# One block of products, one difference, one unit's keys and a range-check step in another place of the order (HGRN2 attention and a maxout FFN on one core)

## The chip, the cores and the metric

The kernel runs on one core of one Trainium2 chip. The metric is the device time of one execution in microseconds (us). The engines named below are PE (TensorE: matmuls, with its weight loads shown apart as PEld), DVE (VectorE), ACT (ScalarE), POOL (GpSimd) and SP (SyncE, which here only issues DMAs).

## The reference, cut to what matters

```python
# q, k, v, f_logit: (4, 8, 768, 48)
f = 1.0 / (1.0 + np.exp(-f_logit))
for t in range(S):
    state = f[:, :, t, :, None] * state + einsum('bhd,bhe->bhde', k[:, :, t], v[:, :, t])
    y[:, :, t] = einsum('bhd,bhde->bhe', q[:, :, t], state)
x = y.transpose(0, 2, 1, 3).reshape(3072, 384)      # tokens x (heads * head_dim)
h = max(max(x @ w1, x @ w2), x @ w3)                # w1..w3: 384 x 768
out = h @ w_out                                     # 768 x 384
```

## The kernel before, in words

**Units and groups.** The attention works in 24 units (u = 0 to 23). A unit is a chunk of 64 time steps of two batches, 128 tokens. Four units make a group of 512 tokens, and there are six groups (g = 0 to 5). The FFN of a group is computed while the attention of the next group runs. `load`, `load_v` and `load_weights` issue the transfers, nearly all on SP's queue.

**One unit of attention.** `sigmoids(u)` makes the gates (ACT). `scan(u)` and `before(u)` run the running products over time (DVE, L329 and L347). `after(u)` and `before(u)` scale keys and queries: `kh` (L340) and `qh` (L351), on DVE for units 0 to 5 and on POOL afterwards. `keys(u)` turns `kh` for the state's sum: for units 0 to 5 that is four PE transposes (L367) into a PSUM bank and an ACT copy to `ks` (L369). For later units `keys_by_blocks` does it on DVE (L382). `pairs(u)` makes the 32 products of keys and queries on PE (L396) and masks them on DVE (L399). `values(u)` multiplies them with v (L415); where u is 4 or more, a tiny ACT copy `seen` (L422) marks that PE is through. `sums(u)` multiplies `ks` with v (L433). `finish(u)` adds the old state's part on PE (L504), which waits for `seen`, and copies the result to the group's `xT` in three ACT copies (L511). `pack` moves pieces of `xT` to other partitions by DMA.

**The FFN in portions.** `fill(ns)` takes steps of the pending FFN generator until their stated cost is used up. So the order on each engine is written out by hand: a few FFN steps, then a step of the attention, and so on. Every engine runs its own instructions in that order.

**The FFN of groups 1 to 5**, `inputs_by_pairs(g, hm, xT)`, works on 256 columns of two weight blocks at once (index n = 0, 1, 2) in the manner of a Winograd-Strassen product, with sums and differences of weights (made once) and of tokens. `sums_of_x(g)` makes the five differences t1 to t5 of tokens on POOL (L865). The steps concerned here all use a helper `into` (L881), whose call makes two 128x256 fp32 matmuls, which the trace shows as four records:

- `start(n)`: one `into` in a new bank A[n] from the pool that the trace calls "p"; ACT copies it to `first` (L895, shown as rest_bits).
- `plain(n)`: two `into` in a new bank B[n] from the pool "tr"; ACT copies it to `out(n, 0)`, columns of `hm` (L889). Both pools have two banks.
- `join(n)`: POOL adds `first` to `out(n, 0)` (L899).
- `sixth(n)`: adds one `into` to A[n]; ACT copies it to `out(n, 1)` (L909).
- `fifth(n)`: starts B[n] anew with one `into`; ACT copies it to a tile `top` (L904).
- `seventh(n)`: adds two `into` to A[n]; ACT copies it (L916, shown as top_bits), POOL adds `top` (L917).
- `third(n)`, `fourth(n)`: further products into B[n] and A[n], read by DVE (L924; L931 and L932).

After them `outputs_by_pairs` makes the output products (L636), with two "tr" banks and one "p" bank. Its last DVE read of a "tr" bank is L644. `store_late()` puts the stores of the group before on SP's queue.

**The FFN of group 0**, `ffn_first`, rounds and prepares the weights as it goes. In its output part it makes four differences of `w_out` columns on POOL: `mix(0)` to `mix(3)` (L592). `mix(1)` overwrites columns of `w_out` that the plain output products of group 0 still read.

**The range check.** From unit 10 on, `check_range(n, step)` checks one loaded weight piece on ACT in three steps: step 0 takes absolute values (L278), steps 1 and 2 compare and add up (L280 and a read of the accumulator). In the loop over units its three steps are spread over the unit's portions.

Of the kernel before, what the change touches and what calls it, by code (L numbers as in the profile page):

```python
# [55 lines left out]
def kernel(  # L56
# [21 lines left out]
    GRP = 4  # L78
# [11 lines left out]
    def fast():  # L90
        ctx = ExitStack()
        with ctx:
# [704 lines left out]
            def ffn_first(xT):  # L797
                hm = new_hm()
                steps = [(j, slice(n * HALF, (n + 1) * HALF)) for n in range(2) for j in range(J_HALF)]
                steps += [(j, slice(0, TOK)) for j in range(J_HALF, NJ)]  # L800
                n_step = 0
                for j, t in steps:
                    w = t.stop - t.start
                    for i in (1, 2):
                        p = yield from product(xT, j, i, t)
                        if i == 1:
                            nc.scalar.copy(hm[:, j, t], p)
                        else:
                            nc.vector.scalar_tensor_tensor(hm[:, j, t], hm[:, j, t], 0.0, p, op0=ALU.max, op1=ALU.max)
                        round_to(ROUNDED[n_step])  # L810
                        load_weights(2, rounded[0] - 1)
                        yield (1 if w == TOK else NK) * w * COLUMN
                        n_step += 1
                        if n_step in TURNED:
                            yield from turn(TURNED[n_step])
                for a in range(NK):
                    if a < 2:
                        for n in range(2 * NK + 2):
                            place(placed[a].bitcast(FP32), w_in[a + 1], n)
                    for cost in linear(a):  # L820
                        round_to(rounded[0] + 1)
                        yield cost
                for n in range(2 * NK + 2):
                    place(w_lin, w_nat, n)
                made = iter([lambda n=n: mix_in(n) for n in range(4)] + [lambda: mix(0)])
                for i in range(GRP):
                    for n, cost in enumerate(outputs(hm, xT, i)):
                        if i or n:
                            next(made, lambda: None)()
                        if i == GRP - 1 and n == 1 and 1 in packed:  # L830
                            sums_of_x(1)
                        if i == GRP - 1 and n == 2:
                            for k in range(1, 4):
                                mix(k)
                        yield cost

# [15 lines left out]
            packed, summed = {}, {}  # L852
# [3 lines left out]
            def sums_of_x(g):  # L856

                if g not in summed:
                    xT = packed[g]
                    X = lambda k, h: halves(xT, k, h)  # L860
                    t1, t2, t3, t4, t5 = (halves(xT, NK, 0), halves(xT, NK, 1), s_mix[0][:, HJ - 1],
                                          rests[:, 2, 0:HALF], s_mix[1][:, HJ - 1])
                    for dst, x, y in ((t1, X(0, 1), X(0, 0)), (t2, X(1, 1), t1), (t3, X(1, 1), X(0, 1)),
                                      (t4, X(1, 0), t2), (t5, X(2, 0), X(2, 1))):
                        nc.gpsimd.tensor_tensor(dst, x, y, op=ALU.subtract)  # L865
                    summed[g] = t1, t2, t3, t4, t5
                return summed[g]

            def inputs_by_pairs(g, hm, xT):
                X = lambda k, h: halves(xT, k, h)  # L870
                t1, t2, t3, t4, t5 = sums_of_x(g)
                s1, s2, s4 = w_sum
                s3 = w_two[1][:, 0]
                COST = 2 * HALF * COLUMN
                out = lambda n, h: hm[:, 2 * n:2 * n + 2, h * HALF:(h + 1) * HALF]
                first, u3 = rests[:, 0:2, 0:HALF], tops[:, 2:4, 0:HALF]
                A, B, U5 = {}, {}, {}

                def into(b, n, w, x, begin=False):
                    for j in range(2):  # L880
                        nc.tensor.matmul(b[:, j * HALF:(j + 1) * HALF], lhsT=w[:, (2 * n + j) * 128:(2 * n + j + 1) * 128],  # L881
                                         rhs=x, start=begin and j == 0, stop=True, skip_group_check=True)

                def plain(n):
                    B[n] = bank(True)
                    into(B[n], n, w_two[0][:, 1], X(1, 0), True)
                    yield COST
                    into(B[n], n, w_two[0][:, 2], X(2, 0))
                    nc.scalar.copy(out(n, 0), two(B[n]))  # L889
                    yield COST  # L890

                def start(n):
                    A[n] = bank()
                    into(A[n], n, w_two[0][:, 0], X(0, 0), True)
                    nc.scalar.copy(first, two(A[n]))  # L895
                    yield COST

                def join(n):
                    nc.gpsimd.tensor_tensor(out(n, 0), out(n, 0), first, op=ALU.add)  # L899

                def fifth(n):
                    into(B[n], n, s1, t1, True)
                    U5[n] = two(new_top(TOK))
                    nc.scalar.copy(U5[n], two(B[n]))  # L904
                    yield COST

                def sixth(n):
                    into(A[n], n, s2, t2)
                    nc.scalar.copy(out(n, 1), two(A[n]))  # L909
                    yield COST  # L910

                def seventh(n):
                    into(A[n], n, s3, t3)
                    yield COST
                    into(A[n], n, w_two[1][:, 2], X(2, 1))
                    nc.scalar.copy(u3, two(A[n]))  # L916
                    nc.gpsimd.tensor_tensor(u3, u3, U5[n], op=ALU.add)  # L917
                    yield COST

                def third(n):  # L920
                    into(B[n], n, s4, X(1, 1))
                    yield COST
                    into(B[n], n, w_two[0][:, 2], X(2, 1))
                    nc.vector.tensor_tensor(out(n, 1), two(B[n]), out(n, 1), op=ALU.add)  # L924
                    yield COST

                def fourth(n):
                    into(A[n], n, w_two[1][:, 1], t4)
                    yield COST
                    into(A[n], n, w_two[1][:, 2], t5)  # L930
                    nc.vector.scalar_tensor_tensor(out(n, 0), out(n, 0), 0.0, two(A[n]), op0=ALU.max, op1=ALU.max)  # L931
                    nc.vector.scalar_tensor_tensor(out(n, 1), out(n, 1), 0.0, u3, op0=ALU.max, op1=ALU.max)  # L932
                    sums_of_hm(hm, n)
                    if g == 1:
                        for i in ((0, 1), (2, 3, 4), ())[n]:
                            mix_x(i)
                    yield COST

                yield from start(0)
                yield from plain(0)  # L940
                join(0)
                store_late()
                yield from sixth(0)
                yield from fifth(0)
                for n in range(1, NJ // 2):
                    yield from plain(n)
                    yield from seventh(n - 1)
                    yield from start(n)
                    join(n)
                    yield from third(n - 1)  # L950
                    yield from fifth(n)
                    yield from sixth(n)
                    yield from fourth(n - 1)
                yield from seventh(NJ // 2 - 1)
                yield from third(NJ // 2 - 1)
                yield from fourth(NJ // 2 - 1)
# [35 lines left out]
            with tc.manual_schedule():  # L992
# [78 lines left out]
                for u in range(GRP, NU):  # L1071
# [2 lines left out]
                    if n == BY_ROWS:  # L1074
                        scan(n)
                    fill(part)
                    keys(u)
                    keys_by_blocks(u, 2)
                    room_of_unit = room_of_pairs()
                    if u > GRP:  # L1080
                        values(u - 1)
                        sums(u - 1, room_of_unit)
                    pairs(u, room_of_unit)
                    if u > GRP:
                        finish(u - 1, xT)
# [17 lines left out]
                    if n < NU:  # L1103
                        if n < BY_ROWS:
                            sigmoids(n)
                        if n != BY_ROWS:
                            scan(n)
                    check_range(u - CHECKS, 0)
                    fill(part)
                    if n < NU:  # L1110
                        after(n)
                        before(n)
                    fill(part)
                    if BY_ROWS < u + 2 < NU and u % GRP == 0:
                        load(u + 2, one, "k")
# [289 lines left out]
```

## Time and profile before

| | us |
|---|---|
| median of 3 runs (lowest to highest) | 415.52 (415.32 to 416.43) |
| the profiled execution | 416.13 |
| its span, first to last instruction | 414.4 |
| PE busy, DVE busy, POOL busy, ACT busy | 393.5, 295.1, 246.0, 180.4 |
| granted PE clock, mean | 0.999 |
| one group in the steady part (182.4 to 241.3, 241.3 to 300.2) | 58.9 |

A busy time adds up an engine's instructions; matmul records overlap, so a busy PE is not a PE at its peak. "Idle before" and "waited for" name the instruction that released the waiting one, as the profile infers it from semaphore events. The "chain" is followed back from the last instruction, at each step to what released it.

### The profile page before, as it was taken

Reading aid. Unit: us, or ns where it says so; the run is one execution under the profiler, and the core shown is the slowest. Engines: PE = TensorE matmul, PEld = TensorE weight load, DVE = VectorE, ACT = ScalarE, POOL = GpSimd, SP = SyncE. Lnnn points to the kernel's source line nnn. Section 1 sums busy time; section 2 is a strip of 40 time slices with the busy share of each in tenths; the row PEclk is TensorE's granted clock in tenths of the full one; section 3 lists DMA queues with packets and bytes.
Section 4 is the critical chain, followed back from the end, with each engine's and each line's share of the span. In section 5 each row is a group of like instructions: output and inputs, shape, how many; then the busy total and the mean of one; then the engine's idle time right before and its main releaser. Section 6 shows DMA issues by size and latency. Waiting matters only on the chain.

```text
span 414.4 us, 11516 instructions
## 1 busy us (share of the span) xinstructions
PE 393.5 (95%) x4598; PEld 331.8 (80%) x4598; DVE 295.1 (71%) x569; ACT 180.4 (44%) x430; POOL 246.0 (59%) x270
## 2 busy tenths in 40 slices
PE   5988999999999989999999999999999999999995
PEld 4766765556667878998889988899988889988994
DVE  6997896997785899898899997998995550002600
ACT  2488786421223522335532345532445424586110
POOL 2189694830969777567495296577377860435700
PEclk9999999999999999999999999999999999999999
DMA  8999886676356766277645276735374003542002
GB/s 168 238 271 272 246 228 90 85 139 161 84 103 99 122 108 124 57 96 114 114 123 109 43 112 85 148 87 89 60 144 110 2 17 88 133 133 72 0 21 62
DMA packets 181562, 47.21 MB, mean 114 GB/s; under 512 B 160448, under 2 KB 179200, under 8 KB 181504
## 3 DMA queue, kind: packets, MB, share of 16 engines
q1 hardware_dynamic: 178032, 45.62, 54.1%
q10 hardware_dynamic: 3472, 0.81, 0.9%
q8 instruction: 37, 0.61, 0.6%
q14 instruction: 21, 0.17, 0.1%
HBM read 37.75 MB, written 4.72 MB: 102 GB/s over the span
## 4 chain that ended last, share of the span: by engine, by line
PE 74%; SPq 6%; POOL 5%; DVE 5%; ACT 4%; issue 2%; DMA 2%; POOLq 0%
PE p L881 15%; PE p L636 14%; PE tr L881 12%; PE tr L636 10%; PE p L542 7%; PE p L568 3%; PE p L787 3%; PE y L415 2%; SPq L164 2%; SPq L174 2%; DVE ks L382 2%; PE y L504 2%; PE a L396 2%; PE a L433 2%; POOL w_in L258 1%
## 5 line engine op out<-in xcount | busy, mean ns | idle before, releaser
L382 DVE STREAM_TRANSPOSE ks<-kh 32x128 f32<-32x128 f32 x256 | 77.4, 302 | 13.4 <-POOL kh L340 9.4
L881 PE MATMUL tr<-xT,placed 128*128 128x256 f32 x300 | 71.5, 383 | 1.1 <-ACT hm L889 1.1
L881 PEld LDWEIGHTS tr<-xT,placed 128*128 128x128 f32 x300 | 56.0, 190 | 10.4 <-ACT hm L889 2.6
L881 PE MATMUL p<-xT,placed 128*128 128x256 f32 x180 | 44.8, 380 | 1.1 <-POOL xT L865 0.8
L339 POOL COPY ends<-r 128x8 f32<-128x8 f32 x24 | 8.8, 366 | 51.1 <-DVE r L329 51.1
L881 PEld LDWEIGHTS p<-xT,placed 128*128 128x128 f32 x180 | 33.9, 190 | 6.4 <-POOL xT L865 1.2
L542 PE MATMUL p<-xT,w_in 128*128 128x256 f32 (+1 forms) x108 | 34.0, 459 | 3.4 <-POOL w_in L756 1.9
L329 DVE TENSOR_TENSOR_SCAN r<-gate,from_one 128x520 f32<-128x520 f32 x24 | 32.5, 1354 | 6.1 <-ACT gate L308 2.8
L340 POOL TENSOR_TENSOR kh<-kt,r 128x512 f32<-128x512 f32 x18 | 30.9, 1715 | 7.6 <-DVE kt L296 7.6
L511 ACT COPY xT<-y 64x256 f32<-64x256 f32 (+1 forms) x60 | 22.1, 368 | 23.2 <-PE y L504 22.5
L347 DVE TENSOR_TENSOR_SCAN prod<-gate,from_inv 128x520 f32<-128x520 f32 x24 | 31.5, 1312 | 0.0
L608 POOL TENSOR_TENSOR w_in<-hm 128x256 f32<-128x256 f32 x15 | 11.1, 739 | 32.2 <-DVE hm L932 29.4
L644 DVE TENSOR_TENSOR o<-tr,w_in 128x384 f32<-128x384 f32 (+1 forms) x11 | 5.7, 521 | 34.3 <-PE tr L636 29.8
L881 PE MATMUL p<-w_in,placed 128*128 128x256 f32 x120 | 30.0, 379 | 0.0
L542 PEld LDWEIGHTS p<-xT,w_in 128*128 128x128 f32 x108 | 19.5, 190 | 12.6 <-issue 6.0
L924 DVE TENSOR_TENSOR hm<-tr,hm 128x512 f32<-128x512 f32 x15 | 10.3, 684 | 23.1 <-ACT raw L280 17.2
L258 POOL TENSOR_TENSOR w_in<-top_bits,rest_bits 128x384 uint32<-128x384 uint32 x18 | 21.9, 1223 | 7.2 <-DVE top_bits L252 3.8
L636 PE MATMUL p<-w_in,hm 128*128 128x192 f32 x120 | 25.3, 334 | 0.6 <-ACT w_in L641 0.6
L641 ACT COPY w_in<-p 128x384 f32<-128x384 f32 x15 | 7.2, 478 | 42.1 <-PE p L636 42.1
L280 ACT ACTIVATE raw<-top_bits 128x384 f32<-128x384 f32 x48 | 25.2, 526 | 0.4
L881 PEld LDWEIGHTS p<-w_in,placed 128*128 128x128 f32 x120 | 22.8, 190 | 3.1
L636 PE MATMUL tr<-w_out,w_in 128*128 128x192 f32 x120 | 24.4, 326 | 0.0
(156 smaller groups left out, 913.7 us busy)
## 6 DMA issues: line engine op xcount, KB each, us to landing
raw<-in_moe_w_dram SPq DMA_DIRECT2D x24, 384.0 KB, 4.3
v_ld<-in_v_dram SPq DMA_DIRECT2D x48, 96.0 KB, 3.3
placed<-in_moe_w_dram SPq DMA_DIRECT2D x12, 384.0 KB, 5.7
out_dram<-o SPq DMA_DIRECT2D x46, 96.0 KB, 2.2
placed<-in_moe_w_out_dram SPq DMA_DIRECT2D x6, 384.0 KB, 5.4
f_ld<-in_f_logit_dram SPq DMA_DIRECT2D x36, 64.0 KB, 2.6
k_ld<-in_k_dram SPq DMA_DIRECT2D x36, 64.0 KB, 2.5
q_ld<-in_q_dram SPq DMA_DIRECT2D x36, 64.0 KB, 2.5
```

Of the source, the lines that this page charges most:

```text
L258: nc.gpsimd.tensor_tensor(dst, by(top), by(rest), op=ALU.add)
L280: nc.scalar.activation(over, size, AF.Relu, scale=(-1 / HI_MIN, 1.0)[step - 1], bias=(1.0, -HI_END * (1 - 2.0 ** -24))[step - 1], accum_ou ...
L329: nc.vector.tensor_tensor_scan(r[:, 0:LEN][:, ::-1], flat(gate)[:, ::-1], flat(from_one)[:, ::-1], 1.0, op0=ALU.mult, op1=ALU.max)
L340: (nc.vector if u < BY_ROWS else nc.gpsimd).tensor_tensor(kh.rearrange("p h a t -> p a h t"), kt, by_batch(r[:, 1:LEN + 1].rearrange("p (x ...
L347: nc.vector.tensor_tensor_scan(flat(prod), flat(gate_tiles[u % 2]), flat(from_inv[u % 2]), 1.0, op0=ALU.mult, op1=ALU.max)
L382: nc.vector.transpose(ks[n * 32:(n + 1) * 32, :, par, e0:e0 + 32], kh[p0:p0 + 32, :, a, t0:t0 + 32])
L511: nc.scalar.copy(xT[o, :, t0 + a * C:t0 + (a + 1) * C], y[i, a, 0:HP * C].rearrange("p (h t) -> p h t", h=HP))
L542: nc.tensor.matmul(p if w < TOK else p.rearrange("p (two t) -> p two t", two=2), lhsT=w_in[i][:, kt, j * 128:(j + 1) * 128], rhs=x[:, t.st ...
L568: nc.tensor.matmul(p[:, 0:DM], lhsT=lhsT, rhs=rhs, start=(n == 0), stop=(n == NJ + NK - 1))
L636: nc.tensor.matmul(b[:, p * HD:(p + 1) * HD], lhsT=x, rhs=w, start=id(b) not in begun, stop=True, skip_group_check=True)
L787: nc.tensor.matmul(p[:, 0:DM], lhsT=w_in[0][:, a, j * 128:(j + 1) * 128], rhs=w_out[:, j, :], start=(j == 0), stop=(j == NJ - 1))
L881: nc.tensor.matmul(b[:, j * HALF:(j + 1) * HALF], lhsT=w[:, (2 * n + j) * 128:(2 * n + j + 1) * 128], rhs=x, start=begin and j == 0, stop= ...
```

## The change

Four pieces change place in the written order. Nothing is computed otherwise.

1. In `inputs_by_pairs`, `plain(1)` comes directly after `plain(0)`, `join(0)` and `store_late()`, ahead of `sixth(0)` and `fifth(0)`; before, it came after them.
2. In `ffn_first`, `mix(1)` is made one step earlier, ahead of `sums_of_x(1)`.
3. In the loop over units, `keys(u)` comes after `values(u - 1)` and `sums(u - 1)` instead of ahead of them. `keys` does something for u = 4 and 5 only in this loop, and for u = 4 there are no values and sums between.
4. `check_range(u - CHECKS, 0)` comes one portion and the calls `after(n)`, `before(n)` later.

```diff
-                        if i == GRP - 1 and n == 1 and 1 in packed:
-                            sums_of_x(1)
+                        if i == GRP - 1 and n == 1:
+                            mix(1)
+                            if 1 in packed:
+                                sums_of_x(1)
                         if i == GRP - 1 and n == 2:
-                            for k in range(1, 4):
+                            for k in range(2, 4):
                                 mix(k)
...
                 yield from plain(0)
                 join(0)
                 store_late()
+                yield from plain(1)
                 yield from sixth(0)
                 yield from fifth(0)
                 for n in range(1, NJ // 2):
-                    yield from plain(n)
+                    if n > 1:
+                        yield from plain(n)
                     yield from seventh(n - 1)
                     yield from start(n)
                     join(n)
...
                     fill(part)
-                    keys(u)
                     keys_by_blocks(u, 2)
                     room_of_unit = room_of_pairs()
                     if u > GRP:
                         values(u - 1)
                         sums(u - 1, room_of_unit)
+                    keys(u)
                     pairs(u, room_of_unit)
...
-                    check_range(u - CHECKS, 0)
                     fill(part)
                     if n < NU:
                         after(n)
                         before(n)
+                    check_range(u - CHECKS, 0)
                     fill(part)
```

## The prediction

> **What bounds the kernel now.** First the page: engines, then the chain of work that ended last.
>
> ```profile
> span 414.4 us, 11516 instructions
> ...
> PE 393.5 (95%) x4598; PEld 331.8 (80%) x4598; DVE 295.1 (71%) x569; ACT 180.4 (44%) x430; POOL 246.0 (59%) x270
> ...
> PE 74%; SPq 6%; POOL 5%; DVE 5%; ACT 4%; issue 2%; DMA 2%; POOLq 0%
> ```
>
> TensorE is the bound where the chain runs on it. The chain in order of time says where that is: from about 38 to 109 us and from 163.4 us to the end it is almost only PE; between 109 and 163.4 us it goes over SP's issues, DMAs, POOL and DVE. So a saved PE wait is worth its length in the first and last stretch only, and the first counts only if the middle lets it through. Next, the waits of the weight loads:
>
> ```profile
> PEld tr L881 <- ACT hm L889: 2.6, 4, 0.8
> PEld y L504 <- ACT seen L422: 2.5, 2, 1.7
> PEld p L881 <- POOL xT L865: 1.2, 1, 1.2
> PEld p L881 <- ACT rest_bits L895: 0.7, 1, 0.7
> ```
>
> Columns: total us, times, longest. These four are the waits that the diff touches. The first is `fifth(0)`, once in each of groups 2 to 5. The timeline of group 2:
>
> ```profile
> 186.39 1.13 ACT L511 COPY xT<-y 128x256 f32<-128x256 f32 x3 [1.23 <-PE y L504]
> ...
> 187.01 0.84 PEld L881 LDWEIGHTS p<-xT,placed 128*128 128x128 f32 x4
> 187.22 1.03 PE L881 MATMUL p<-xT,placed 128*128 128x256 f32 x4
> ...
> 187.54 0.56 ACT L278 ACTIVATE top_bits<-raw 128x384 f32<-128x384 f32 x1
> 188.01 0.57 ACT L889 COPY hm<-tr 128x512 f32<-128x512 f32 x1
> 188.47 0.59 ACT L909 COPY hm<-p 128x512 f32<-128x512 f32 x1
> 188.63 0.94 PEld L881 LDWEIGHTS tr<-xT,placed 128*128 128x128 f32 x5 [0.78 <-ACT hm L889]
> ```
>
> `fifth(0)` restarts the bank that `plain(0)` filled, so it waits for ACT's copy L889; that stands behind three xT copies (L511) and the range check's L278. The timeline of the middle stretch:
>
> ```profile
> 123.18 1.53 POOL L865 TENSOR_TENSOR xT<-xT 128x256 f32<-128x256 f32 x2 [3.74 <-DMA xT<-xT]
> ...
> 124.77 0.73 PEld L881 LDWEIGHTS p<-xT,placed 128*128 128x128 f32 x4 [1.22 <-POOL xT L865]
> ...
> 129.86 4.15 SPq L183 DMA_DIRECT2D q_ld<-in_q_dram  x8
> ...
> 136.17 0.71 DVE L296 STREAM_TRANSPOSE qt<-q_ld 128x512 f32<-128x512 f32 x1 [1.81 <-DMA out_dram<-o]
> ...
> 155.57 0.52 PEld L504 LDWEIGHTS y<-qh,state 48*48 48x48 f32 x32 [1.66 <-ACT seen L422]
> ...
> 163.41 0.30 PEld L636 LDWEIGHTS p<-w_out,hm 128*128 128x128 f32 x2 [0.99 <-DVE hm L931]
> ```
>
> The reader is to see a pin. SP issues back to back from 58 to 155.4 us (pauses of some 0.05 us, none over 0.5): its queue waits for nothing, so the q transfer of 129.86 lands when it lands, and DVE takes it at 136.17. From there DVE is busy to 163.4 us with one pause of 0.33 us (for POOL, itself behind DVE's kt). PE waits for this chain at 138.20 (0.45, POOL qh), 155.57 and 163.41 us.
>
> **What the Trainium skill says.** "TensorE: Matmul & The Clock Gate", Step-by-step: weight loads are pulled ahead of running matmuls, matmuls stay in program order. The trace agrees: a load stands 0.21 us ahead of its matmul (187.01 and 187.22), and a waiting matmul holds all behind it. "Perfetto Trace Analysis", Matmuls: independent groups should rotate through PSUM banks so that one is evacuated under the next one's matmuls. This case's trace has the opposite at 188.63, where the bank just filled is needed again four matmul records later. The same page, What "DMA-bound" means: a solid row of DMA slices on the issuing sequencer is a bound of its own. SP's row agrees for 58 to 155 us.
>
> **The change part by part.** No instruction is added or removed; the order on DVE and SP is the same, on PE, ACT and POOL some stand elsewhere.
>
> (a) *plain(1) ahead of sixth(0) and fifth(0), groups 1 to 5.* Eight matmul records (12 take 2.59 us in the chain, so 0.216 each, 1.73 in all) now stand between the last of `plain(0)` and `sixth(0)`. Removed: in group 2 the load after the line of 187.22 was due at 187.22 + 4 x 0.216 = 188.08 for the matmul, which came at 188.63: 0.54; and the twelve after it take 2.86 instead of 2.75 (the line of an unbroken twelve), 0.11 for the restart. Groups 3 and 4 (246.16 to 247.56, 305.09 to 306.49) give the same 0.54 + 0.11; group 5 (361.61 to 362.50) 0.03 + 0.11. Sum 3 x 0.65 + 0.14 = 2.09 us. The cover of L889 is now 1.73 + 0.86 us of matmuls, against 0.86.
>
> What is late next: `seventh(0)`. It adds to the bank that `sixth(0)` filled and waits for the copy L909. Before, `fifth(0)` and `plain(1)` lay between (12 records, 2.59 us); now only `fifth(0)` (4, 0.86). Let P be the start of the last record of `plain(1)`. The last of `sixth(0)` starts at P + 0.86 and takes 0.38; ACT starts some 0.04 later, P + 1.28, if free, runs 0.585, and PE's load follows 0.05 later (188.01 + 0.57 to 188.63): P + 1.915. The load is due with the last record of `fifth(0)`, P + 1.73. Late by 0.185. In group 5's old wait a load 0.25 late (362.25 to 362.50) cost PE 0.14, in group 2 0.755 late cost 0.65: 0.11 is absorbed. Cost 0.075 where ACT is free.
>
> The bank that `plain(1)` takes is the other "tr" bank, last read by DVE's L644 (183.05 to 183.6 in group 2); it is asked for at about 187.0 instead of 188.6 us. 3.4 us of room: cost nothing. `hm`'s columns for n=1 were last read before the final 2 us of the outputs: nothing.
>
> (b) *Range check's L278 a portion later.* It leaves the place ahead of L889 and, by the order of ACT's instructions in groups 2 to 4, comes between the second L889 and L909. ACT starts successive copies 0.46 to 0.47 apart (187.54, 188.01, 188.47). Second L889 at P + 0.41, L278 at P + 0.88, L909 at P + 1.35 instead of 1.28: `seventh(0)` is 0.255 late, cost 0.145 in groups 2 to 4. In group 5 L278 falls behind L909: 0.075. L280 follows later as before; nobody waits for it. By itself (b) would have taken 0.46 off the old wait; with (a) that wait is gone, so (b) is worth minus 0.07 a group.
>
> (c) *keys(5) behind values(4) and sums(4).*
>
> ```profile
> 67.52 0.59 ACT L369 COPY ks<-tr 128x512 f32<-128x512 f32 x1
> 67.99 0.14 ACT L422 COPY seen<-y 1x1 f32<-1x1 f32 x1
> 68.19 0.52 PEld L504 LDWEIGHTS y<-qh,state 48*48 48x48 f32 x32 [0.85 <-ACT seen L422]
> ```
>
> ACT's `seen` no longer stands behind ks: 67.52 instead of 67.99, so the wait at 68.19 shrinks by 0.47 us. `ks` itself is first used at 80.7. Four transposes only change place. On the span: nothing, because of the pin at 136.17. Bounds: 0 to 0.47.
>
> (d) *mix(1) ahead of the sums, POOL.* One L592 (1.40 us) moves into POOL's wait of 3.74 us before 123.18 (its w_out columns are free once the last outputs have read them, about 117 us). The join L899 of 132.00 starts 1.4 us sooner, so does ACT's L895, and most of PE's 0.67 at 133.94 goes. In group 1, (a) also covers the wait of 124.77 (1.09 with its restart). Together about 1.4 us of PE before 138.2. It then waits at 138.20, 155.57 and 163.41 for DVE, as before: value 0, bounds 0 to 1.9 with (c). SP's packs and stores keep their order, and SP was full anyway.
>
> **Sum** against the profiled run (span 414.4, time 416.13, 1.73 us around the span): groups 2 to 4, 3 x (0.65 - 0.145) = 1.515; group 5, 0.14 - 0.075 = 0.065; group 1 and unit 5, 0. 416.13 - 1.58 = 414.55. The profiled run stands 0.61 above the median of the runs, 415.52; I take the same saving off that: **413.9 us**, 0.38% less. A measurement of this kernel can tell about 0.3%, 1.25 us, from no change. That DVE follows PE's gain is seen in group 2: it waits for PE 1.49 us at 199.36 and 0.34 at 211.06.
>
> **Rivals.**
> 1. *The middle gives way too* (the pin is looser than I read it): up to 1.85 more, 412.1. For: POOL's L865/L592 are on the chain from 123 to 133. Against: DVE's 1.81 and 4.43 us waits for transfers. Chance 0.09.
> 2. *The gain is eaten by late partners*: `seventh(0)` waits longer, or DVE's L932 (222.00 to 222.68 in group 2, its reader's load at about 222.88: 0.15 of room) does not follow. Gain 0.4 to 1.1: 414.4 to 415.1. Chance 0.24.
> 3. *Slower*: ACT. If behind the second L889 not only L278 but also an L280 with its accumulator read (0.53 + 0.19) ran before L909, `seventh(0)` would lose 0.145 + 0.7 against the 0.65 saved: 3 x 0.2 lost, 416.1; it decides from one more ACT instruction of 0.5 us on. The written order puts L280 behind, so 0.07 for this and any like it.
> 4. *It does nothing*: PE order unchanged. The order lists exclude it.
> My forecast keeps 0.60: 413.4 to 414.4.
>
> Faster by over 0.3% (below 414.27): most of the forecast's 0.60 (0.55) and rival 1's 0.09: 0.64. Within: 0.05 + 0.22 = 0.27. Slower by over 0.3%: 0.09, rival 3 and the rest of rival 2. Range: 413.1 (no wait at `seventh(0)` and a little of the middle) to 415.1 us (rival 2's end).
>
> **What would show it.** Right: no wait on L889 in groups 2 to 5; a new wait of `seventh(0)` on ACT L909 (weight loads idle about 0.2 to 0.3); group spacing 58.9 us down to about 58.4; PE's restart still at 163.4 us; the wait on `seen` at 68 us about 0.4. Wrong: a restart in the middle earlier than 163.1, or a group spacing that stays at 58.9.

## The result and the profile after

| kernel | median, us | range | runs |
|---|---|---|---|
| before | 415.47 | 413.06 to 416.66 | 20 |
| after | 413.98 | 411.92 to 415.59 | 20 |

The ratio is 0.9968, 95% interval 0.9954 to 0.9981: 0.3% faster, 1.5 us. The profiled execution of the changed kernel has a span of 411.9 us and a time of 413.64. Lines 834 to 942 of before stand 2 further down (L881 is L883, L889 is L891, L909 is L911); L278, L296, L351, L422 and L504 keep their numbers.

The page of the changed kernel, span and chain:

```profile
span 411.9 us, 11516 instructions
...
PE 84%; DVE 5%; DMA 4%; POOL 2%; issue 2%; ACT 2%; SPq 0%; ACTq 0%; DVEq 0%; POOLq 0%
```

The spans differ by 2.5 us, the medians by 1.5. So the two profiled executions can't simply be subtracted; which part of 2.5 us is the change's is worked out below. Next the waits of the weight loads (total us, times, longest), those that answer to the four of before:

```profile
PEld y L504 <- ACT seen L422: 1.7, 1, 1.7
PEld p L883 <- issue: 1.3, 4, 0.3
```

Of the four lines only `seen` is left, with the long one of its two waits. `fifth(0)`'s wait for L889 (2.6 us, four times) is gone. Where it stood there is one of four times 0.3 us for which the profile sees no releaser ("issue"); the timeline of group 2 shows what it is:

```profile
187.58 0.84 PEld L883 LDWEIGHTS p<-xT,placed 128*128 128x128 f32 x4
...
187.99 0.58 ACT L891 COPY hm<-tr 128x512 f32<-128x512 f32 x1 [1.02 <-PE tr L883]
...
188.44 0.84 PEld L883 LDWEIGHTS tr<-xT,placed 128*128 128x128 f32 x4
...
188.47 0.56 ACT L278 ACTIVATE top_bits<-raw 128x384 f32<-128x384 f32 x1
188.94 0.57 ACT L911 COPY hm<-p 128x512 f32<-128x512 f32 x1
...
189.62 0.73 PEld L883 LDWEIGHTS p<-w_in,placed 128*128 128x128 f32 x4 [0.34 <-issue]
```

`fifth(0)`'s loads (188.44) follow those of `sixth(0)` (187.58) without a bracket: nothing is waited for. `seventh(0)`'s load of 189.62 stands idle 0.34 us. The bracket says "issue", but the copy that it needs, L911, ends at 188.94 + 0.57 = 189.51, just ahead of it. ACT's order is L891 of `plain(1)`, then L278, then L911: the order of the prediction.

What a group takes is read from the distance between the same matmul (the first L415 after the inputs) in successive groups. These times are read to 0.01 us, so a distance can be off by 0.01. The table of windows, first of before, then of after; columns: window and its length, then busy time and count of PE, PE's weight loads, DVE, ACT and POOL, then granted clock, DMA share and GB/s:

```profile
199.19:258.12 58.93, 58.55 (x774) 53.20 (x773) 52.89 (x111) 24.49 (x60) 37.92 (x40) 1.00 0.56 98
```

```profile
197.59:256.09 58.50, 58.50 (x774) 53.26 (x773) 52.44 (x111) 24.38 (x61) 37.92 (x40) 1.00 0.57 100
```

The same 774 matmul records in 58.50 instead of 58.93 us; PE's busy time now equals the window. The next group says the same: 58.92 before, 58.49 after.

Unit 5 and the middle stretch of the changed kernel, in the timeline:

```profile
67.51 0.14 ACT L422 COPY seen<-y 1x1 f32<-1x1 f32 x1
67.56 0.57 ACT L369 COPY ks<-tr 128x512 f32<-128x512 f32 x1
67.70 0.52 PEld L504 LDWEIGHTS y<-qh,state 48*48 48x48 f32 x32
```

```profile
134.56 0.71 DVE L296 STREAM_TRANSPOSE qt<-q_ld 128x512 f32<-128x512 f32 x1 [2.68 <-DMA out_dram<-o]
...
135.34 1.18 POOL L351 TENSOR_TENSOR qh<-qt,prod 128x512 f32<-128x512 f32 x1 [2.49 <-DVE qt L296]
...
136.57 0.56 PEld L396 LDWEIGHTS a<-qh,kh 48*64 48x64 f32 x32 [0.84 <-POOL qh L351]
```

`seen` now runs ahead of ks, and PE follows. Then at 134.56 everything hangs on a DMA again, as at 136.17 before: DVE waits 2.68 us for the q transfer, POOL for DVE, PE for POOL. (The bracket names a store, which uses the same DMA semaphore as one of the q transfers and lands at 134.70, too late to be the releaser; the last of the eight q transfers lands at 134.43, before it was 136.05 against a start of 136.17.) That this came 1.6 us earlier is not the change's doing: SP's queue was already 1.2 us ahead at about 50 us, ahead of any instruction that the change moves.

**Where the time came from.** PE's place against before, in this pair of profiles: 1.15 us ahead at 164 to 183 us; group 2 adds 0.44, group 3 0.435, group 4 0.43; group 5 adds nothing (from unit 21's values to the start of the last matmul 92.05 us after, 92.04 before). The three groups are the change's, 1.30 us, beside 1.5 in the medians. The 1.15 at 164 us belongs to this execution: 1.6 us from SP's place, less some 0.45 lost to a spell of lower clock. Windows of the changed kernel, same columns:

```profile
150.00:156.00 6.00, 4.45 (x137) 3.60 (x136) 5.48 (x12) 1.86 (x6) 5.92 (x7) 0.92 0.78 191
156.00:160.00 4.00, 4.00 (x17) 3.61 (x16) 3.85 (x10) 1.04 (x3) 3.67 (x6) 0.70 0.34 65
```

In the second window PE has 17 records in 4 us at a granted clock of 0.70. PE comes to `p<-w_out,hm` after that, so late that the wait for DVE which stood at 163.41 us before is not there in this profile.

### The profile page after: what moved, and what is told of

It is laid out like the page before. It is cut to its first block, busy times and chain, and to the rows that moved or that the text cites. A ratio compares the mean times of both kernels' runs of the same rounds, so it can differ in the third digit from the quotient of the medians.

```text
span 411.9 us, 11516 instructions
## 1 busy us (share of the span) xinstructions
PE 393.1 (95%) x4598; PEld 333.0 (81%) x4598; DVE 293.7 (71%) x569; ACT 180.3 (44%) x430; POOL 245.8 (60%) x270
## 4 chain that ended last, share of the span: by engine, by line
PE 84%; DVE 5%; DMA 4%; POOL 2%; issue 2%; ACT 2%; SPq 0%; ACTq 0%; DVEq 0%; POOLq 0%
PE p L883 17%; PE p L636 15%; PE tr L883 15%; PE tr L636 11%; PE p L568 6%; PE p L542 6%; PE p L787 3%; PE y L415 3%; PE a L396 3%; PE y L504 2%; PE a L433 2%; DMA placed<-in_moe_w_dram 1%; DMA k_ld<-in_k_dram 1%; DVE ks L382 1%; DVE r L329 1%
## 5 line engine op out<-in xcount | busy, mean ns | idle before, releaser
L883 PE MATMUL tr<-xT,placed 128*128 128x256 f32 x300 | 71.1, 382 | 0.0
L883 PEld LDWEIGHTS tr<-xT,placed 128*128 128x128 f32 x300 | 56.5, 190 | 7.8
L883 PE MATMUL p<-xT,placed 128*128 128x256 f32 x180 | 44.6, 379 | 0.0
L339 POOL COPY ends<-r 128x8 f32<-128x8 f32 x24 | 7.8, 326 | 51.2 <-DVE r L329 51.2
L883 PEld LDWEIGHTS p<-xT,placed 128*128 128x128 f32 x180 | 34.2, 190 | 4.6
L340 POOL TENSOR_TENSOR kh<-kt,r 128x512 f32<-128x512 f32 x18 | 31.9, 1771 | 8.1 <-DVE kt L296 8.1
L883 PE MATMUL p<-w_in,placed 128*128 128x256 f32 x120 | 31.2, 391 | 0.0
L883 PEld LDWEIGHTS p<-w_in,placed 128*128 128x128 f32 x120 | 23.0, 195 | 4.6 <-issue 1.3
```

Of the source, the lines that this page charges most:

```text
L340: (nc.vector if u < BY_ROWS else nc.gpsimd).tensor_tensor(kh.rearrange("p h a t -> p a h t"), kt, by_batch(r[:, 1:LEN + 1].rearrange("p (x ...
```

## The experiments

The two theories. **Mine**: after the pin (the q transfer that DVE takes at about 135 us) every saved PE wait is worth its length, ahead of it nothing; (a) saves 0.65 us a group and pays part of it back at `seventh(0)`, (b) costs 0.07 on top of (a), (c) and (d) are worth 0. **Rivals**: the middle gives way and the saving is partly that of (c) and (d); or the saving is (b)'s and (a) only moves the wait; or the whole difference is SP's scatter. "Distance" is that of a group, as above. Each ratio is against runs of the kernel before on the same chip.

| kernel | median, us (runs) | ratio, 95% interval | distance, us |
|---|---|---|---|
| before | 415.28 to 415.59 | 1 | 58.93, 58.92 |
| e1_plain: (a) alone | 414.12 (22) | 0.997, 0.9957 to 0.9982 | 58.43, 58.42 |
| e2_check: (b) alone | 414.09 (21) | 0.9972, 0.9957 to 0.9987 | 58.49, 58.49 |
| e3_keys_mix: (c), (d) alone | 415.01 (14) | 0.9995, 0.998 to 1.001 | 58.93, 58.94 |
| e4_no_check: all but (b) | 414.12 (22) | 0.9965, 0.9951 to 0.9978 | 58.43, 58.42 |
| after: all | 413.98 (20) | 0.9968, 0.9954 to 0.9981 | 58.50, 58.49 |
| e5_sixth | 413.16 (7) | 0.9958, 0.9941 to 0.9974 | 58.28, 58.29 |
| e6_stores | 434.06 (5) | 1.0449, 1.0424 to 1.0474 | 58.50, 58.49 |
| e7_sixth_stores | 434.37 (5) | 1.0463, 1.0438 to 1.0488 | 58.29, 58.28 |
| e8_late | 410.39 (6) | 0.988, 0.9856 to 0.9903 | 58.50, 58.50 |
| e9_sixth_late | 409.73 (6) | 0.9878, 0.984 to 0.9916 | 58.28, 58.30 |
| e10_before_late | 411.9 (6) | 0.9917, 0.9897 to 0.9937 | 58.94, 58.93 |

The medians of the small differences are not separated from one another (e1, e2, e4, after); the distances, which agree within 0.02 us in one profile, are.

**e1_plain**, before with (a) alone:

```diff
                 store_late()
+                yield from plain(1)
                 yield from sixth(0)
                 yield from fifth(0)
                 for n in range(1, NJ // 2):
-                    yield from plain(n)
+                    if n > 1:
+                        yield from plain(n)
```

> The kernel before with edit (a) alone: plain(1) ahead of sixth(0) and fifth(0). Theory (seventh's new wait is one ACT copy plus the hand-over to PE): L278 now runs ahead of the first L889, L909 stands behind nothing, so seventh(0) loses about 0.14 us and a group gains 0.65 - 0.14 = 0.51. Distance of the first values products of two successive groups in the steady part 58.93 before, 58.42 here. Time against before: -1.5 us. Rival (the saving comes from L278's move, not from plain(1)): 58.93, no gain.

Measured: 58.43, a gain of 0.50 a group. (a) alone makes the whole difference, and a little more than all four edits.

**e2_check**, before with (b) alone:

```diff
-                    check_range(u - CHECKS, 0)
                     fill(part)
                     if n < NU:
                         after(n)
                         before(n)
+                    check_range(u - CHECKS, 0)
```

> The kernel before with edit (b) alone: L278 a portion later. Theory: L889 starts 0.47 us earlier, fifth(0) is 0.29 instead of 0.755 us late, of which 0.11 is absorbed, so a group gains 0.47 and the steady distance is 58.46; time -1.4 us. This would mean that (b) alone brings nearly what the whole change brings. Rival (L278 is not what holds L889; the xT copies are): 58.93, no gain.

Measured: 58.49, a gain of 0.44. `fifth(0)` still waits, but less. The timeline of group 2:

```profile
187.42 2.46 PEld L881 LDWEIGHTS tr<-xT,placed 128*128 128x128 f32 x12 [0.33 <-ACT hm L889]
```

0.33 us idle instead of 0.78. So either edit alone brings nearly all of it, and the two do not add: they shorten the same wait, one by putting matmuls into it, one by taking 0.46 us of ACT out of it.

**e3_keys_mix**, before with (c) and (d) alone:

```diff
-                        if i == GRP - 1 and n == 1 and 1 in packed:
-                            sums_of_x(1)
+                        if i == GRP - 1 and n == 1:
+                            mix(1)
+                            if 1 in packed:
+                                sums_of_x(1)
...
-                    keys(u)
                     keys_by_blocks(u, 2)
...
                         sums(u - 1, room_of_unit)
+                    keys(u)
```

> The kernel before with edits (c) and (d) alone: keys(5) behind values and sums, mix(1) ahead of the sums. Theory (the middle is pinned to the q transfer on SP's queue): PE is 0.48 us earlier from 70 to 109 us, its pairs of unit 9 start 2.03 us after DVE's transpose of that q and its wait near 163 us ends 27.2 us after it, as before; steady distance 58.93; time 0, within 0.3. Rival 1 (the middle gives way): 0.5 to 1.9 us faster.

Measured: no change of distance and none of time that 14 runs can see; the interval of the ratio, 0.998 to 1.001, still leaves room for a gain of 0.8 us. In the profile, (c) does what it says: from L779 to L504 PE takes 3.20 us before (64.99 to 68.19) and 2.73 here (65.41 to 68.14); (d) does too: the wait on `rest_bits` near 134 us is gone from the list. This execution came there 0.42 us late, so the 0.48 us of lead that was expected shows as 0.05. From 138 us on PE stands 0.86 us ahead, which is what qt is ahead (135.31 against 136.17), whatever PE had gained before. The wait for DVE near 163 us, which was expected as before, is missing, because a spell of low clock (see the last section) had put PE behind DVE.

**The pin in seven kernels.** From DVE's start on qt to PE's load after its long wait (155.57 us before) it is 19.41 or 19.42 us in each of before, after, e1, e2, e3, e4 and e5, while qt itself starts anywhere from 134.30 (e5) to 137.47 us (e4):

| | before | after | e1 | e2 | e3 | e4 | e5 |
|---|---|---|---|---|---|---|---|
| qt starts | 136.17 | 134.56 | 136.78 | 135.40 | 135.31 | 137.47 | 134.30 |
| PE restarts | 155.58 | 153.97 | 156.20 | 154.81 | 154.73 | 156.88 | 153.72 |

Its place follows no edit in these seven executions, one of each kernel: e4, which has (a), (c) and (d), comes last, and e3 comes ahead of before. Single executions scatter by 3 us here, and so the distance is the sharper measure.

**e4_no_check**, after without (b):

```diff
+                    check_range(u - CHECKS, 0)
                     fill(part)
                     if n < NU:
                         after(n)
                         before(n)
-                    check_range(u - CHECKS, 0)
```

> The changed kernel without edit (b): L278 where it was. Theory: L278 runs ahead of the first L889, whose lateness is now covered, and L909 follows the second L889 at once, so seventh(0) is 0.07 us less late: steady distance 58.42 against 58.49, time 0.2 us below the changed kernel. Rival ((a) and (b) add up): distance 58.49 + 0.44 = 58.93.

Measured: 58.43, so (b) costs 0.07 a group where (a) is there. ACT in group 2 of e4:

```profile
188.85 0.56 ACT L278 ACTIVATE top_bits<-raw 128x384 f32<-128x384 f32 x1
...
191.32 0.59 ACT L911 COPY hm<-p 128x512 f32<-128x512 f32 x1 [0.28 <-PE p L883]
```

L278 is done long before L911, and L911 now waits for PE's last `sixth(0)` matmul instead of for ACT. That it runs 0.07 sooner is the 0.07.

**e5_sixth**, after with `sixth(0)` ahead of `plain(1)`, so that each of the two banks has 12 matmul records between its fill and its next use:

```diff
-                yield from plain(1)
                 yield from sixth(0)
+                yield from plain(1)
                 yield from fifth(0)
```

> The changed kernel with sixth(0) ahead of plain(1): plain(0), sixth(0), plain(1), fifth(0), seventh(0). Now eight matmul records and more lie between either bank's last product and its next use. Theory: both waits are covered, a group gains the whole 0.65, steady distance 58.28 against 58.93 before and 58.49 with the change; group 5 gains 0.14; time 0.8 us below the changed kernel, 2.1 below before. Rival (the wait left at seventh(0) is not the bank's copy but something else that it waits for): distance stays 58.49.

Measured: 58.28, the whole 0.65 a group. Group 2 of e5, ACT and then the weight loads:

```profile
186.13 0.59 ACT L891 COPY hm<-tr 128x512 f32<-128x512 f32 x1
186.87 0.59 ACT L911 COPY hm<-p 128x512 f32<-128x512 f32 x1 [0.15 <-PE p L883]
```

```profile
189.05 0.84 PEld L883 LDWEIGHTS p<-w_in,placed 128*128 128x128 f32 x4
```

L911 ends at 187.46, and `seventh(0)` asks for its bank at 189.05: no bracket, no wait. It is the order that the Trainium skill, "Perfetto Trace Analysis", Matmuls, describes (a bank is evacuated under the next bank's matmuls), and the trace agrees with it: 0.21 us a group against the order of the change.

**e6_stores** and **e7_sixth_stores** were to take the pin away: after (e7: e5) with the eight stores of group 0's outputs issued from ACT's queue.

```diff
-            def store(u, o):
+            def store(u, o, queue=nc.sync):
...
-                    nc.sync.dma_start(out=out[t0:t0 + C, :], in_=o[a * C:(a + 1) * C, :])
+                    queue.dma_start(out=out[t0:t0 + C, :], in_=o[a * C:(a + 1) * C, :])
...
-                            store(i, o)
+                            store(i, o, nc.scalar)
```

> The changed kernel, with the eight stores of group 0's outputs issued from ACT's queue instead of SP's. Six of them stand on SP ahead of the q transfer that the middle waits for, at about 0.64 us each. Theory (the middle is pinned to SP's queue): DVE's transpose of that q comes up to 3.8 us earlier, PE's waits near 136 (0.9) and 152 us (1.76) shrink or go, and the time falls by 1.5 to 3 us against the changed kernel; steady distance stays 58.49. Rival (the pin is the transfers themselves or PE, not SP's issues): 0, within 0.3.

> Both: sixth(0) ahead of plain(1) and the stores of group 0 from ACT's queue. Theory: the two savings lie in different stretches and add: 0.8 us from the groups (steady distance 58.28) and 1.5 to 3 us from the middle, 3.5 to 5 us below the kernel before. Rival: the later groups' saving is lost again to DVE once the middle is quicker, 2 us below before.

Measured: 4.5% slower, both. SP's waits, and PE's, in e6:

```profile
SPq L458 <- DMA out_dram<-o: 16.3, 1, 16.3
```

```profile
PE a L396 <- POOL qh L351: 15.9, 1, 15.9
```

SP, which had waited for nothing, waited 16.3 us for a store that it had not issued. The trace shows the link: the DMAs of SP and ACT use eight DMA semaphores in turn, and each issue waits for the one that it uses. The SP issue of 101.88 us uses the semaphore of ACT's store of 99.45, which landed at 101.86; so a store late on ACT's queue holds an SP issue that was written after it. As a test of the pin both failed: they took away SP's solid row and put a worse wait there. They show one thing: with everything ahead of 163 us upset by 18 us, the distances are still 58.50 and 58.29.

**e8_late** was to do the same without another queue: after with the same stores on SP, but written behind the next group's k, q and f transfers.

```diff
-                            store(i, o)
+                            late.append((i, o))
...
                 join(0)
-                store_late()
+                if g > 1:
+                    store_late()
...
+                    if g == 1 and n == 1:
+                        store_late()
```

(The last two lines stand behind the first `fourth()` of group 1.)

> The changed kernel with the eight stores of group 0's outputs still on SP's queue, but moved behind the k, q and f transfers of the middle (written after the first fourth() of group 1). Six of them stood ahead of the q transfer, 0.64 us each, 3.8 in all. Theory (the middle is pinned to SP's queue): DVE's transpose of that q comes up to 3.8 us earlier, PE's waits near 136 (0.9) and 152 us (1.76) shrink or go; time 1.5 to 3 us below the changed kernel; steady distance stays 58.49. Rival (the pin is PE or the transfers themselves, not the queue's length): within 0.3 of the changed kernel.

Measured: 410.39 us, 0.988 of before. Page and SP's timeline of e8:

```profile
span 407.9 us, 11517 instructions
...
PE 89%; SPq 3%; DMA 2%; POOL 2%; DVE 1%; issue 1%; ACT 1%; POOLq 0%
```

```profile
123.06 5.32 SPq L183 DMA_DIRECT2D q_ld<-in_q_dram  x8
...
146.91 5.54 SPq L560 DMA_DIRECT2D out_dram<-o  x8
```

The q issue begins at 123.06 us, against 128.21 in the changed kernel's profile (129.86 before), and the eight stores stand behind it at 146.91. DVE starts on qt at 130.96 instead of 134.56 us. PE has no gap between 78 and 185 us, and the chain is almost PE alone from 60 to 200 us. So it was the q transfer behind SP's other issues that set the middle, and moving eight stores is worth 3.6 us against the changed kernel's median, more than twice the change itself and more than the 1.5 to 3 us expected.

**e9_sixth_late**, the same three edits on e5:

> Both: sixth(0) ahead of plain(1), and the stores of group 0 behind the transfers. Theory: the savings lie in different stretches and add: 0.8 us from the groups (steady distance 58.28) and 1.5 to 3 us from the middle; 3.5 to 5 us below the kernel before. Rival: the later groups' saving is lost to DVE once the middle is quicker; about 2 us below before.

Measured: 409.73 us, the best median of all and 5.65 us below before, where 3.5 to 5 were expected; but its runs (408.78 to 413.97) do not separate it from e8's (409.12 to 411.5). In the profiles its last matmul starts at 402.51 us, e8's at 402.62, although the three groups are 0.21 shorter each. Some 0.8 us went back at 158 us, where PE stood twice for DVE. Its weight loads, then DVE in e8 and in e9:

```profile
158.90 0.30 PEld L636 LDWEIGHTS p<-w_out,hm 128*128 128x128 f32 x2 [0.55 <-DVE hm L933]
...
159.50 0.30 PEld L636 LDWEIGHTS p<-w_out,hm 128*128 128x128 f32 x2 [0.30 <-DVE hm L934]
```

```profile
157.48 0.68 DVE L933 SCALAR_TENSOR_TENSOR hm<-hm,p 128x512 f32<-128x512 f32 x1
```

```profile
158.17 0.68 DVE L933 SCALAR_TENSOR_TENSOR hm<-hm,p 128x512 f32<-128x512 f32 x1
```

DVE's maxout (L933, L934) is what is late. It looks like rival 2 (DVE follows with little room), but PE had gained only 0.13 us on e8 by then, while DVE is 0.69 us later than in e8. That is the q transfer again: qt starts at 131.64 us in e9 and at 130.96 in e8, and from qt to L933 (L931 before the change) DVE takes 26.50 to 26.53 us in before, after, e1 to e5 and e8 to e10. So moving the stores starts this chain of DVE's early enough that PE hardly waits for it; the chain itself stays, and a late q transfer shows at once.

**e10_before_late**, the three edits on the kernel before, to see what the change is worth where there is no pin:

> The kernel before with the stores of group 0 moved in the same way. Theory: the pin goes here too, 2 to 3 us below before; but now the old waits at 68, 124 and 134 us count, so this kernel stands 2.5 to 3.2 us above the changed kernel with moved stores, instead of the 1.3 to 1.5 that the change is worth with the pin. Rival (those waits are hidden anyway, pin or not): 1.3 to 1.5 us above it.

Measured: 411.9 us, 1.5 above e8, not the 2.5 to 3.2 expected. By the medians it is the rival that came true (1.3 to 1.5: those waits are hidden anyway), though six runs of each can hardly tell 1.5 from 1.8. In the profiles the last matmul starts at 404.39 against 402.62 us, 1.77 apart: 1.31 are the three groups, 0.49 the `seen` wait of (c), which still stands at 68 us in e10, and some 0.1 comes in group 1, less 0.16 by which e10's PE was ahead of e8's at 65 us. What is missing against the forecast are the waits of 124 and 134 us, for which I had counted (a) in group 1 and (d). POOL in e10, timeline:

```profile
120.02 1.54 POOL L865 TENSOR_TENSOR xT<-xT 128x256 f32<-128x256 f32 x2 [1.05 <-ACT o L572]
```

POOL's L865 begins at 120.02 instead of 123.18 us and waits for ACT, no longer for the pack: SP issues the pack (L524) at 115.67, since the stores do not stand ahead of it. So these waits were SP's queue as well, and go when the stores do, whether or not (a) and (d) are there.

## Why the prediction was right, and where it was off

- **The time**: 413.9 us forecast, 413.98 measured. The sum was 1.58 us; the groups gave 1.30 in the trace, the medians differ by 1.5. That the medians agree to 0.1 us is partly luck, since they can't tell 1.3 from 1.6.
- **(a), the wait removed**: right. The 0.65 us a group (0.54 of load, 0.11 of restart) is what e5 shows when nothing is paid back: 58.93 to 58.28.
- **(a), the new wait of `seventh(0)`**: right in place and cause, mis-sized. The term was 0.145 a group with L278 in between; measured 0.65 - 0.44 = 0.21. With P = 187.576, ACT's three starts were forecast for P + 0.41, 0.88 and 1.35, and came at 0.41, 0.89 and 1.36. The step that failed is "PE's load follows 0.05 later", taken from L889 in the old wait. Here the load came at 189.62, 0.11 after the copy's end at 189.51: a semaphore instruction of 0.051 us, for ACT, stands ahead of the load at 189.55, and the load itself waits for POOL. In the old wait the load had ACT alone to wait for and no such instruction ahead of it. The same 0.11 stands in groups 3 and 5 and in e4. The load due at P + 1.73 was 0.31 late; with 0.11 absorbed that is 0.20, as measured. e4 confirms it with the other size: 0.075 + 0.06 = 0.135 expected so, 58.43 - 58.29 = 0.14 measured.
- **Group 5**: forecast 0.065, measured 0.00. The same 0.06 to 0.07 of hand-over eats it: 0.14 saved, 0.14 paid. e5 gets 0.13 there.
- **(b)**: right. Minus 0.07 a group behind (a) (e4), 0.44 by itself (e2) where 0.46 was said.
- **(c)**: `seen` came 0.48 us earlier (0.47 forecast) and PE with it. No wait is left, where about 0.4 was forecast, because the transposes now fill that time. In the time nothing of it is seen (e3, within 0.8 us). That it is hidden rather than lost rests on one pair of profiles, e10 against e8: 0.49 us once the stores are out of the way.
- **(d)**: value 0, as forecast, but half the reason was wrong: I treated the waits of 124 and 134 us as POOL's and ACT's own, to be saved by 1.4 us of POOL. They too hang on SP's queue: in e10 both are gone without (d).
- **The pin**: shown. 19.41 us from qt to PE's restart in seven kernels, and PE's waits in the middle going in e8 when q is issued earlier. Rival 1 (the middle gives way) finds no support: the middle of the profile of after is 1.6 us earlier, but SP's queue was ahead from before the change acts, and e3 with (c) and (d) alone gains no time, within its 0.8 us. As a sign I had named an absolute time (a restart ahead of 163.1 us); by that sign the profile of after, where PE comes to this place at 162.64 us, would speak against the forecast. It was badly chosen, since SP's scatter moves it by more than the effect.
- **Rival 2** happened in its first half only: `seventh(0)` waits longer than forecast, by 0.06 us a group. DVE did not fail to follow in groups 2 to 5, since e1, e4 and e5 kept all that PE saved. **Rival 3** needs a second ACT instruction behind L891; the timeline has only L278 there.

## What to carry to other kernels

Between two uses of a PSUM bank put the fill of other banks, and check every bank of the rotation: the change freed one and left the next with 4 matmul records of cover, while one more exchange of two lines frees both. Two edits that shorten one wait do not add, so price the second with the first in place. And before saving PE waits ahead of a transfer, look at what stands ahead of that transfer in its issue queue: moving eight stores behind it brought more than all four edits, and only then did a saving ahead of it begin to count (0.49 us, in one pair of profiles).

## What was not expected of the hardware

- A load that waits for two engines (ACT and POOL) came 0.11 us after the copy's end, where one that waited for ACT alone came 0.05 after it; the profile calls the idle time of the first "issue", so that it is missing from the list of waits on ACT.
- After PE's wait at about 154 us (weight loads idle for 1.69 us), matmul records in after, e3 and e5 stood 0.427 us apart instead of 0.216 for about 3 us; the traces give a granted clock of 0.5 for 3.41 us there. In after this cost some 0.45 us. Before, e1, e2 and e4 have nearly the same wait (1.66 to 1.69 us) and no such spell, and e8, e9 and e10 have neither. e3 has one more, at 29.5 us, and e6 and e7 have long ones (17.1 and 13.7 us) behind PE's waits of 15.9 and 14.9 us. It is not the change's: the mean clock is 0.996 to 0.997 over the runs of before and 0.996 over those of after. What sets off the short ones stays open.
- SP's queue, with nothing to wait for, reached the same issue up to 3 us apart in executions of kernels that give it the same work in the same order.
